# A three-part kernel on one core: queries read as whole rows of 18 tokens, keys and values in 96 partitions, weight tiles of 256 columns

## The chip, the cores and the metric

The kernel runs on one core of a Trainium2 chip. The metric is the device time of one execution in microseconds (us), and the time of a kernel is the median of its runs.

## The reference

An attention without softmax, then two feed-forward layers, over 8 batches, 8 heads, 576 tokens and 64 features (4608 tokens of 512 features). The weights are float64 in memory.

```python
kv  = einsum('bhsd,bhse->bhde', k, v)
out = einsum('bhsd,bhde->bhse', q, kv)
out = out / sqrt(mean(out * out, -1) + 1e-6) * g_norm
x   = out.transpose(0, 2, 1, 3).reshape(B * S, H * D)
h   = maximum(maximum(x @ w1, x @ w2), x @ w3)      # 512 -> 768
x   = h @ w_out                                     # 768 -> 512
g   = s * maximum(x @ w_in, 0) ** 2 + b             # 512 -> 2048
out = g @ w_out2                                    # 2048 -> 512
```

## The kernel before

**Tiling.** Tokens go in nine blocks of 512: block j below 8 holds the first N = 512 tokens of batch j, and the ninth holds the 8 x 64 tokens that are left (REM = 64 of each batch, gathered in `o_rem`). Features lie on partitions, tokens on the free axis. Heads go in four pairs p: heads p and p + 4 fill 128 partitions.

**Attention of one batch.** `load_kv` reads the first 512 tokens of k and v of a pair into 128 partitions of 4 tokens (pieces of 1 KB), `load_rem` the last 64 of all heads into `krem` and `vrem`; `kv_mm` sums k-by-v products into the PSUM tile `kvps`, 10 matmuls a pair, the last two from `krem` and `vrem`. `load_q` reads q as blocks of 32 x 32, which one DVE transpose (`q_turn`) turns into `qt`, features by tokens. Then come q times kv (`o_mm`, PSUM `ops`, `orps` for the last 64 tokens), copy and square on ACT (`o`, `sq`), the mean square (`ms_mm`), `u` on ACT and DVE (`ms_ln`, `ms_newton`), and the split of the result into a high and a low part `xh`, `xl` (`x_split`), since each product of the feed-forward layers is made of three matmuls (`mm3`).

**First layer.** 18 tiles of W1 to W3 and 6 of `w_out` are loaded as raw float64 words (`conv_load`, buffers `raw_craw` and `raw_o`) and turned into high and low parts `w_w` in three steps (`conv_unpack`, `conv_sum`, `conv_split`) on DVE, ACT and POOL. Group g (`g1_part`) multiplies a block by 128 columns of one of W1, W2, W3; three groups and a maximum make one tile of h (`g1_out`, `h_split`), and `g2_mm` multiplies h by `w_out`. The result `x1d` goes to device memory.

**Second layer.** Phase 2 runs on quarters of tokens with fewer products than a plain multiplication. `put` turns the result back into rows of tokens and stores it. For the last pair of the quarters (`qq == NQ - 1`, the tokens of `o_rem`) TensorE turns it (PSUM `turn`) and eight DMAs of 64 tokens store it, six issued by SP and two by ACT; all others go out in DMAs of 32 tokens in four parts of 128 features.

**Order.** Each step gets a position with `at(pos, step)`; a slot of the steady part is one group. SP and PE follow the positions (PE from the steady part on); the order on DVE, ACT and POOL is a scheduler's. All loads and nearly all stores are issued by SP, in order. In the start-up, the attention of batch 0, the tiles of W and the products of block 0 come together; from block 1 on the attention of the next batch runs beside the products of a block.

Of the kernel before, what the change touches and what calls it, by code (L numbers as in the profile page):

```python
# [9 lines left out]
F32 = mybir.dt.float32  # L10
# [19 lines left out]
def attention_max_ffn_relu2_ffn(ctx: ExitStack, tc, q, k, v, g_norm, w1, w2, w3, wo, wi, w2o, s, b, out):  # L30
# [21 lines left out]
    M2 = DF2 // P  # L52
    REM = S - N
    NB = B + 1
    C = N // P
    SB = S // 32
    G1 = 3 * M1
    SL = G1 + KD
    ts = nc.vector.tensor_scalar
# [5 lines left out]
    def at(pos, fn, *args):  # L65
        plan.append((pos, len(plan), fn, args))
# [15 lines left out]
    def pair(slot, nm):  # L82
        return base.tile([P, 2, N], F32R, tag=slot, name=nm)
# [52 lines left out]
    rems = {}  # L136
    for nm in "kv":
        rems[nm] = at_.tile([P, H, D], F32, name=f"{nm}rem")
        nc.gpsimd.memset(rems[nm], 0.0)
# [34 lines left out]
    def stage(raw, tr, gc):  # L174

        def parts():
            if gc == "st":
# [15 lines left out]

    def conv_split(key, slot, eng):
        f = st.pop(("f32", key))
        w = wt[key] = pair(slot, f"w_{key[0]}_{key[1]}")
        split(w[:, 0], w[:, 1], f, eng)

    def conv_store(key):
        nc.sync.dma_start(out=wd[key[1] // 4][:, key[1] % 4], in_=st.pop(("f32", key)))  # L200

    def w1_src(n):
        m, i = divmod(n, 3)
        w = (w1, w2, w3)[i][:, m * P:(m + 1) * P]
# [15 lines left out]

    def load_rem(bb):
        for nm, src in (("k", k), ("v", v)):
            nc.sync.dma_start(out=rems[nm][:REM], in_=src[bb, :, N:, :].rearrange("h r d -> r h d"))

    def load_kv(bb, p):
        for nm, src in (("k", k), ("v", v)):
            tag = (nm, 2) if bb or p < 2 else ("o", NP)
            t = st[nm, bb, p] = at_.tile([P, 2, C, D], F32, tag=tag[0], bufs=tag[1], name=f"{nm}_{bb}_{p}")  # L230
# [35 lines left out]
    def load_q(bb, p0, n):


        if p0 == 0:
            st["qraw"] = at_.tile([P, NP, SB, 32], F32, tag="qraw", name=f"qraw_{bb}")  # L270
        for j in range(P // 32):
            h = (j // 2) * NP + p0
            src = q[bb, h:h + n, :, (j % 2) * 32:(j % 2 + 1) * 32].rearrange("h (i t) f -> t (h i) f", t=32)
            nc.sync.dma_start(out=st["qraw"][j * 32:(j + 1) * 32, p0:p0 + n].rearrange("t h i f -> t (h i) f"), in_=src)

    def q_turn(bb, p):
        t = st["qt", p] = at_.tile([P, S], F32, tag="qt", bufs=2, name=f"qt_{bb}_{p}")
        nc.vector.transpose(t, st["qraw"][:, p].rearrange("p i f -> p (i f)"))
# [166 lines left out]
    for j in range(NB):  # L445
        t = SL * j
        if j + 1 < B:
            bb = j + 1
            xpb = 3 if j else 2
            if bb < 4:  # L450
                kt = us(4 + 15 * bb)
                plan_kv(bb, lambda p: kt + (2 * p - 3.9) * US, lambda p: kt + 2 * p * US)
            else:
                plan_kv(bb, lambda p: t - 4 + p - 1.9, lambda p: t - 4 + p + 0.5)
            at(max(t - 10, us(20)), load_q, bb, 0, NP)
            at(t + 0.2, kv_diag, bb)
            for p in range(NP):
                a = t + 3 * p
                at(a + 0.4, q_turn, bb, p)
                if bb:  # L460
                    at(a + 1.3, q_split, bb, p)
                at(a + 3.5, o_mm, bb, p)
                at(a + 4.3, o_out, bb, p)
                plan_norm(bb, p, a + 4.5, 0.9)
                at(t + G1 + 0.2 + 0.5 * p, x_split, bb, p, nc.gpsimd if p < xpb else nc.vector)
            at(t + 13.3, o_rems, bb)
        elif j + 1 == B:
            for p in range(NP):
                a = t + 3 * p

                def sq(p=p):
                    st["o", B, p] = o_rem[:, p, :]
                    o_sq(B, p, o_rem[:, p, :])

                at(a + 0.4, sq)
                plan_norm(B, p, a + 0.5, 0.9)
                at(t + G1 + 0.2 + 0.5 * p, x_split, B, p, nc.gpsimd if p < 3 else nc.vector)
        for g in range(G1):
            if j or g >= 4:
                at(t + g, g1_part, j, g, range(KD))  # L480
# [282 lines left out]
    def unit():  # L763
        p2["unit"] = tmp("unit")[:, :P]
        make_identity(nc, p2["unit"])

    def put(H, c, u):

        qq = H // 2
        if qq == NQ - 1:  # L770
# [18 lines left out]

# [87 lines left out]
```

## Time and profile before

| what | value |
| --- | --- |
| median of 3 runs | 1454.68 us (1452.45 to 1455.13) |
| span of the profiled execution | 1453.9 us |
| PE busy | 1396.9 us, 96% of the span |
| DVE busy | 951.2 us, 65% |
| ACT busy | 813.8 us, 56% |
| DMA, mean rate | 139 GB/s |

The profile is of one execution, and its span runs from its first to its last instruction; the run has no time of its own beside it, so the span is taken for it. It lies inside the runs, 0.8 us under the median. PE is TensorE's matmuls, DVE VectorE, ACT ScalarE, POOL GpSimd and SP the engine that issues DMAs. "DMA share" is the busy share of 16 DMA engines (packets that overlap on an engine can make it more than 1).

### The profile page before, as it was taken

How to read it: one execution, taken by the hardware profiler on the slowest of the kernel's cores; microseconds unless marked ns; L12 is line 12 of the kernel's file. 1: busy time of each engine (PE TensorE's matmuls, PEld its weight loads, DVE VectorE, ACT ScalarE, POOL GpSimd, SP SyncE). 2: the span in 40 equal slices, each digit the busy share in tenths (PEclk: the TensorE clock that was granted, in tenths of full speed). 3: DMA queues.
4: the chain of work that ended last, by engine and by line, in shares of the span. 5: the costliest groups of instructions: out<-in, count | busy, mean ns of one | idle time of the engine just before them, and what ended most of it. 6: DMA issues, size and time to landing. Idle time of an engine off the chain costs nothing. (4 is left out here: it accounts for less than half of the span.)

```text
span 1453.9 us, 19580 instructions
## 1 busy us (share of the span) xinstructions
PE 1396.9 (96%) x6860; PEld 1145.0 (79%) x6860; DVE 951.2 (65%) x1439; ACT 813.8 (56%) x1454; POOL 332.7 (23%) x238
## 2 busy tenths in 40 slices
PE   4689999999999999999999999999999999999997
PEld 2467888888878788888878778988788888888887
DVE  4899473646364636446466765756877888888785
ACT  5776454445353545443365646647676666656565
POOL 1334242324232324331100000000002414141412
PEclk9789999999999999999999999999999999999999
DMA  9986244435364742213135464453676444454541
GB/s 195 198 207 106 76 65 111 111 117 102 127 91 124 113 123 58 80 29 116 65 124 202 162 230 178 142 203 127 217 265 231 132 146 174 152 175 148 176 135 40
DMA packets 229459, 202.63 MB, mean 139 GB/s; under 512 B 126320, under 2 KB 179568, under 8 KB 227184
## 3 DMA queue, kind: packets, MB, share of 16 engines
q1 hardware_dynamic: 229200, 201.11, 48.9%
q8 instruction: 54, 0.88, 0.3%
q14 instruction: 45, 0.37, 0.1%
q10 hardware_dynamic: 160, 0.26, 0.0%
HBM read 126.88 MB, written 74.45 MB: 138 GB/s over the span
## 5 line engine op out<-in xcount | busy, mean ns | idle before, releaser
L97 PE MATMUL g<-xl,w_w 128*128 128x512 f32 x648 | 255.9, 395 | 3.8 <-POOL xl L93 3.8
L96 PE MATMUL g<-xh,w_w 128*128 128x512 f32 x648 | 257.4, 400 | 0.2 <-ACT xh L92 0.2
L98 PE MATMUL g<-xh,w_w 128*128 128x512 f32 x648 | 255.6, 395 | 0.0
L92 ACT ACTIVATE zx<-z 128x512 fp32r<-128x512 f32 (+1 forms) x280 | 161.2, 586 | 123.5 <-PE zs_a L707 35.7
L629 PE MATMUL ps_a<-x_q,w_q 128*128 128x512 f32 (+1 forms) x960 | 211.1, 371 | 2.8 <-DVE cs L537 1.7
L707 PE MATMUL zs_a<-zx,w_q 128*128 128x512 f32 (+1 forms) x960 | 203.7, 369 | 0.6 <-POOL zx L93 0.3
L93 POOL TENSOR_TENSOR zx<-z,zx 128x512 fp32r<-128x512 f32 (+1 forms) x46 | 63.3, 1376 | 593.8 <-DMA gd<-cs 381.4
L629 PEld LDWEIGHTS ps_a<-x_q,w_q 128*128 128x128 f32 x960 | 167.2, 188 | 38.0 <-DVE cs L537 3.4
L93 DVE TENSOR_TENSOR zx<-z,zx 128x512 fp32r<-128x512 f32 (+1 forms) x234 | 170.6, 746 | 34.8 <-ACT zx L92 34.3
L707 PEld LDWEIGHTS zs_a<-zx,w_q 128*128 128x128 f32 x960 | 167.8, 188 | 31.9 <-POOL zx L93 0.7
L97 PEld LDWEIGHTS g<-xl,w_w 128*128 128x128 f32 x648 | 123.3, 190 | 29.7 <-POOL xl L93 4.2
L96 PEld LDWEIGHTS g<-xh,w_w 128*128 128x128 f32 x648 | 123.2, 191 | 26.8 <-issue 1.0
L98 PEld LDWEIGHTS g<-xh,w_w 128*128 128x128 f32 x648 | 123.2, 190 | 26.3
L171 POOL TENSOR_TENSOR tr_ctr<-tr_ctr,gc_cgc 128x512 int32<-128x512 int32 x42 | 56.0, 1333 | 232.4 <-DVE gc_cgc L166 169.8
L629 PE MATMUL ps_b<-x_q,w_q 128*128 128x512 f32 (+1 forms) x480 | 107.6, 372 | 1.1 <-ACT cs L640 1.0
L707 PE MATMUL zs_b<-zx,w_q 128*128 128x512 f32 (+1 forms) x480 | 103.8, 371 | 2.2 <-DVE zx L93 2.2
L372 DVE TENSOR_TENSOR h<-g,h 128x512 f32<-128x512 f32 x108 | 73.9, 684 | 42.9 <-PE g L98 42.4
L707 PEld LDWEIGHTS zs_b<-zx,w_q 128*128 128x128 f32 x480 | 83.9, 188 | 19.1 <-DVE zx L93 3.4
L629 PEld LDWEIGHTS ps_b<-x_q,w_q 128*128 128x128 f32 x480 | 83.8, 188 | 18.9 <-ACT cs L640 1.8
L96 PE MATMUL g<-h,w_o 128*128 128x512 f32 x216 | 85.7, 397 | 0.0
L162 ACT ACTIVATE tr_ctr<-raw_craw 128x512 int32<-128x512 uint32 x42 | 28.1, 669 | 102.1 <-DMA wd<-tr_ctr 86.1
L97 PE MATMUL g<-h,w_o 128*128 128x512 f32 x216 | 84.6, 392 | 0.0
(160 smaller groups left out, 2268.3 us busy)
## 6 DMA issues: line engine op xcount, KB each, us to landing
z<-gd SPq DMA_DIRECT2D x64, 512.0 KB
gd<-cs SPq DMA_DIRECT2D x96, 256.0 KB
z<-gd SPq DMA_DIRECT2D x48, 256.0 KB
x1d<-x SPq DMA_DIRECT2D x36, 256.0 KB
k<-in_k_dram SPq DMA_DIRECT2D x32, 256.0 KB
v<-in_v_dram SPq DMA_DIRECT2D x32, 256.0 KB
raw_craw<-in_moe_w_in_dram SPq DMA_DIRECT2D x16, 512.0 KB
wd<-tr_ctr SPq DMA_DIRECT2D x32, 256.0 KB
```

The lines of the kernel that those rows point to most:

```text
L92: act(out=hi, in_=src, func=AF.Copy)
L93: eng.tensor_tensor(out=lo, in0=src, in1=hi.bitcast(F32), op=ALU.subtract)
L96: nc.tensor.matmul(ps, lhsT=w[:, 0, sl], rhs=xh, start=first, stop=False)
L97: nc.tensor.matmul(ps, lhsT=w[:, 0, sl], rhs=xl, start=False, stop=False)
L98: nc.tensor.matmul(ps, lhsT=w[:, 1, sl], rhs=xh, start=False, stop=last)
L162: act(out=r, in_=w32[:, :, 0], func=AF.Copy, scale=2.0 ** -29)
L171: nc.gpsimd.tensor_tensor(out=t, in0=t, in1=g.bitcast(I32), op=ALU.add)
L372: nc.vector.tensor_tensor(out=st["h", m], in0=ps, in1=st["h", m], op=ALU.max)
L629: nc.tensor.matmul(ps, lhsT=w[:, a, c], rhs=x[:, b_], start=new and k == 0 and e == 0, stop=k == HK - 1 and e == 2, skip_group_check=True)
L707: nc.tensor.matmul(ps, lhsT=w[:, a, c], rhs=x[:, b_, :n], start=new and k_ == 0 and e == 0, stop=k_ == 3 and e == 2, skip_group_check=True)
```

## The change

- **Queries.** One DMA for each 32 partitions reads whole rows: partition t gets tokens 18t to 18t + 17 of a head, all 64 features, 4608 bytes on end. Both halves of a head's features are needed in different partitions, so each head is read twice, the copies shifted by 32 columns, and `q_turn` picks 32 of every 64 columns. A load is now for one pair of heads, with two buffers. Tokens thereby lie in the order (c, t) with token = 18t + c, from q to the store.
- **Keys and values.** A pair's 576 tokens lie in 96 partitions of 6 tokens (pieces of 1536 bytes); `load_rem`, its buffers and the memsets on them are gone. `kv_mm` makes 12 matmuls a pair.
- **W1 to W3.** A tile holds 256 columns of half of the inputs (pieces of 2 KB), before 128 columns of all inputs (1 KB). Two groups share two tiles, the groups' order has two tiles of h side by side, and `h_split` comes for two at a time.
- **Stores.** They address memory by `tokens(bb)`, the view (c, t) of a batch: rows of neighbouring t are 18 rows (36,864 bytes) apart. The stores of 32 tokens keep their shape; those of 64 tokens become 2 x 32 rows.

```diff
 def load_kv(bb, p):
-    t = at_.tile([P, 2, C, D], F32, tag=tag[0], bufs=tag[1])
-    nc.sync.dma_start(out=t.rearrange("p h c d -> p h (c d)"),
-                      in_=src[bb, p::NP, :N, :].rearrange("h (p c) d -> p h (c d)", c=C))
+    t = pool.tile([P, 2, CK, D], F32, tag=tag, bufs=bufs)          # CK = 6, KP = 96
+    nc.sync.dma_start(out=t[:KP].rearrange("p h c d -> p h (c d)"),
+                      in_=src[bb, p::NP].rearrange("h (p c) d -> p h (c d)", c=CK))
 def load_q
-    src = q[bb, h:h + n, :, (j % 2) * 32:(j % 2 + 1) * 32].rearrange("h (i t) f -> t (h i) f", t=32)
+    nc.sync.dma_start(out=t[j * 32:(j + 1) * 32, o:o + SB * D],    # o = 32 - 32 * (j % 2)
+                      in_=q[bb, (j // 2) * NP + p].rearrange("(t c) f -> t (c f)", c=SB))
 def w1_src(n)
-    m, i = divmod(n, 3)
-    w = (w1, w2, w3)[i][:, m * P:(m + 1) * P]
+    mp, i, kh = key_of(n)
+    w = (w1, w2, w3)[i][:, 2 * mp * P:2 * (mp + 1) * P]
 def g1_part
-    mm3(..., wt["w", g], slice(kk * P, (kk + 1) * P), ...)
+    c = 2 * (kk % 2) + mm                                          # mp, i, mm = g // 6, g % 6 // 2, g % 2
+    mm3(..., wt["w", (mp, i, kk // 2)], slice(c * P, (c + 1) * P), ...)
+def tokens(bb):
+    return out[bb * S:(bb + 1) * S].rearrange("(t c) f -> c t f", c=SB)
 def put (last pair)
-    eng.dma_start(out=out[r0:r0 + REM], in_=o[e * REM:(e + 1) * REM])
+    eng.dma_start(out=tokens(4 * c + 2 * u + e)[N // 32:], in_=o[e * REM:(e + 1) * REM])
 def put (others)
-    nc.sync.dma_start(out=out[r0:r0 + 32].rearrange("r (a f) -> a r f", a=4), in_=o[:, j])
+    nc.sync.dma_start(out=tokens(2 * qq + c)[4 * u + j].rearrange("r (a f) -> a r f", a=4), in_=o[:, j])
```

On SP, the first loads of batch 0 are these, before (`k_0` and `v_0` are pair 0, `raw_craw` and `raw_o` the tiles of W; the last figures are the shape of one DMA, x4 is four DMAs):

```order
1 L231 DMA k_0_117<-in_k_dram 128x2x256
2 L231 DMA v_0_119<-in_v_dram 128x2x256
3 L225 DMA krem<-in_k_dram 64x8x64
4 L225 DMA vrem<-in_v_dram 64x8x64
5 L274 DMA qraw_123<-in_q_dram 32x18x32 x4
6 L149 DMA raw_craw<-in_moe_w_dram 64x4x128 x2
```

And these in the changed kernel:

```order
1 L228 DMA k_0_113<-in_k_dram 96x2x384
2 L228 DMA v_0_115<-in_v_dram 96x2x384
3 L268 DMA qraw_0_117<-in_q_dram 32x1152 x4
4 L145 DMA raw_craw<-in_moe_w_dram 64x2x256 x2
5 L228 DMA k_1_125<-in_k_dram 96x2x384
6 L228 DMA v_1_127<-in_v_dram 96x2x384
```

The two loads of the last 64 tokens are gone, a q load has pieces of 1152 elements where it had 18 of 32, and a tile of W has two pieces of 256 where it had four of 128.

On PE, where block 0 goes from the last group of the first layer (`g_0_17`) to the products with `w_out` (`g_0_0`, `g_0_1`), the mean square of pair 3 of batch 1 (`ms_3`) stands here before:

```order
278 L96 MATMUL g_0_17_1221<-xh_291,w_w_938 128x512
279 L328 MATMUL ms_3_1218<-sqh_3_1167,ones 128x512
280 L329 MATMUL ms_3_1218<-sql_3_1168,ones 128x512
281 L97 MATMUL g_0_17_1221<-xl_292,w_w_938 128x512
282 L98 MATMUL g_0_17_1221<-xh_291,w_w_938 128x512
283 L96 MATMUL g_0_17_1221<-xh_291,w_w_938 128x512
284 L97 MATMUL g_0_17_1221<-xl_292,w_w_938 128x512
285 L98 MATMUL g_0_17_1221<-xh_291,w_w_938 128x512
286 L96 MATMUL g_0_0_1248<-h_0_701,w_o_990 128x512
```

And here in the changed kernel:

```order
267 L99 MATMUL g_0_17_1261<-xh_296,w_w_973 128x512
268 L97 MATMUL g_0_0_1291<-h_0_782,w_o_1023 128x512
269 L98 MATMUL g_0_0_1291<-h_0_782,w_o_1023 128x512
270 L99 MATMUL g_0_0_1291<-h_0_782,w_o_1023 128x512
271 L97 MATMUL g_0_1_1295<-h_0_782,w_o_1023 128x512
272 L98 MATMUL g_0_1_1295<-h_0_782,w_o_1023 128x512
273 L324 MATMUL ms_3_1258<-sqh_3_1211,ones 128x512
274 L325 MATMUL ms_3_1258<-sql_3_1212,ones 128x512
275 L99 MATMUL g_0_1_1295<-h_0_782,w_o_1023 128x512
```

It had five matmuls of the last group behind it, and has that whole group and five matmuls with `w_out` ahead of it: ten later.

On SP, the last stores of the kernel are these, before (the stores of `o_1_3` are of 32 tokens; those of L781 are of the last pair, 64 tokens each):

```order
580 L788 DMA out_dram<-o_1_2_12113 4x32x128 x4
581 L788 DMA out_dram<-o_1_3_12139 4x32x128 x4
582 L781 DMA out_dram<-o_0_0_12545 64x512 x2
583 L781 DMA out_dram<-o_0_1_12557 64x512 x2
584 L781 DMA out_dram<-o_1_0_12622 64x512
585 L781 DMA out_dram<-o_1_1_12631 64x512
```

And these in the changed kernel:

```order
586 L786 DMA out_dram<-o_1_2_12265 4x32x128 x4
587 L786 DMA out_dram<-o_1_3_12291 4x32x128 x4
588 L780 DMA out_dram<-o_0_0_12697 2x32x512 x2
589 L780 DMA out_dram<-o_0_1_12709 2x32x512 x2
590 L780 DMA out_dram<-o_1_0_12774 2x32x512
591 L780 DMA out_dram<-o_1_1_12783 2x32x512
```

Number and place are as they were, the shape of the last six is another; the two that ACT issues change in the same way.

## Rows read from the trace of the kernel before

**Rows 1.** The page: busy time, share of the span and instructions of each engine.

```profile
PE 1396.9 (96%) x6860; PEld 1145.0 (79%) x6860; DVE 951.2 (65%) x1439; ACT 813.8 (56%) x1454; POOL 332.7 (23%) x238
```

**Rows 2.** Windows by stage: length, busy time by engine; PEclk, DMA share, GB/s.

```profile
0.00:31.30 31.30, 14.81 (x98) 8.85 (x98) 11.37 (x25) 14.24 (x28) 5.53 (x10) 1.00 0.94 189
31.30:73.30 42.00, 25.56 (x147) 16.74 (x147) 35.58 (x51) 30.69 (x53) 13.77 (x10) 0.72 1.10 204
73.30:135.90 62.60, 54.16 (x337) 42.27 (x337) 57.55 (x81) 46.40 (x83) 27.24 (x17) 0.94 0.78 169
135.90:156.60 20.70, 20.68 (x79) 16.85 (x80) 15.37 (x20) 10.00 (x17) 5.53 (x4) 0.86 0.13 34
156.60:1436.00 1279.40, 1270.54 (x6120) 1050.39 (x6120) 826.49 (x1254) 705.49 (x1260) 279.63 (x198) 1.00 0.46 137
```

**Rows 3.** Waits of PE from 145 us on: total us, times, longest.

```profile
PE zs_b L707 <- DVE zx L93: 2.2, 4, 1.4
```

**Rows 4.** Waits of DVE from 0 to 150 us, those for DMA.

```profile
DVE qt L278 <- DMA qraw<-in_q_dram: 12.9, 6, 6.6
DVE gc_o L161 <- DMA raw_o<-in_moe_w_dram: 6.4, 6, 2.4
DVE gc_cgc L161 <- DMA raw_craw<-in_moe_w_dram: 6.0, 4, 2.8
```

**Rows 5.** Timeline of PE, start-up and one batch later: start, us, instructions, idle before.

```profile
102.77 0.34 PE L243 MATMUL kvps<-vrem,krem 128*64 128x64 f32 x4 [3.17 <-DMA vrem<-in_v_dram]
...
135.92 0.79 PE L328 MATMUL ms<-sqh,ones 128*128 128x512 f32 x1 [3.39 <-DVE u L342]
...
156.64 0.39 PE L96 MATMUL g<-xh,w_w 128*128 128x512 f32 x1
156.86 0.39 PE L97 MATMUL g<-xl,w_w 128*128 128x512 f32 x1
...
285.94 0.69 PE L243 MATMUL kvps<-v,k 128*64 128x64 f32 x16
286.46 0.29 PE L243 MATMUL kvps<-vrem,krem 128*64 128x64 f32 x4
```

**Rows 6.** Timeline of DVE: last q_turn of batch 0, last split of block 1's input.

```profile
26.51 0.78 DVE L278 STREAM_TRANSPOSE qt<-qraw 128x576 f32<-128x576 f32 x1 [1.17 <-DMA qraw<-in_q_dram]
...
151.55 0.69 DVE L93 TENSOR_TENSOR xl<-o,xh 128x512 fp32r<-128x512 f32 x1
```

**Rows 7.** Windows of one kind of transfer each; columns as in rows 2.

```profile
103.00:105.00 2.00, 2.00 (x11) 1.60 (x8) 2.00 (x5) 0.59 (x2) 0.00 (x0) 0.77 1.03 378
94.00:96.00 2.00, 2.00 (x11) 1.65 (x10) 1.90 (x4) 1.37 (x4) 0.00 (x0) 1.00 1.07 225
131.00:133.00 2.00, 1.53 (x7) 0.94 (x5) 2.00 (x2) 1.55 (x3) 1.13 (x1) 1.00 1.61 132
156.30:158.30 2.00, 2.00 (x11) 1.65 (x10) 0.00 (x0) 0.36 (x1) 0.00 (x0) 1.00 0.70 255
1199.00:1200.00 1.00, 1.00 (x6) 0.82 (x5) 0.00 (x0) 0.46 (x1) 0.47 (x1) 1.00 1.07 436
1402.00:1406.00 4.00, 4.00 (x36) 4.00 (x35) 2.79 (x9) 2.18 (x6) 0.99 (x1) 1.00 0.28 83
1441.30:1444.00 2.70, 2.45 (x18) 2.15 (x18) 1.43 (x4) 1.82 (x4) 0.00 (x0) 1.00 0.82 191
1450.10:1452.60 2.50, 0.00 (x0) 0.00 (x0) 0.00 (x0) 0.20 (x1) 0.00 (x0) 0.95 0.78 209
```

**Rows 8.** Timeline of the tail: the last stores and the last copy.

```profile
1440.10 10.69 SPq L781 DMA_DIRECT2D out_dram<-o  x6
...
1449.71 0.60 ACT L776 ACTIVATE o<-turn 128x512 f32<-128x512 f32 x1 [0.77 <-PE turn L773]
1450.34 0.50 ACTq L781 DMA_DIRECT2D out_dram<-o  x1
```

More of the change, by code (lines that the diff above doesn't have):

```diff
@@ L54, in attention_max_ffn_relu2_ffn @@
     NB = B + 1
-    C = N // P
     SB = S // 32
+    CK = 6
+    KP = S // CK
     G1 = 3 * M1
@@ L135, in attention_max_ffn_relu2_ffn @@
     o_rem = at_.tile([P, NP, N], F32, name="o_rem")
[L136 to L139, printed above, removed]
     st = {}
@@ L186, in stage, with key_of @@
                 parts)
+    def key_of(n):
+        return ((0, 0, 0), (0, 1, 0), (0, 0, 1), (0, 1, 1))[n] if n < 4 else (n // 6, n % 6 // 2, n % 2)
     W1S = [f"w{n}" for n in range(G1)]
@@ L195, in conv_split @@
         f = st.pop(("f32", key))
-        w = wt[key] = pair(slot, f"w_{key[0]}_{key[1]}")
+        w = wt[key] = pair(slot, f"w_{slot}")
         split(w[:, 0], w[:, 1], f, eng)
@@ L202, in w1_src @@
     def w1_src(n):
-        m, i = divmod(n, 3)
-        w = (w1, w2, w3)[i][:, m * P:(m + 1) * P]
-        return [(h * D, D, w[h * NP * D:(h + 1) * NP * D, :].rearrange("(k d) c -> d k c", d=D)) for h in range(2)]
+        mp, i, kh = key_of(n)
+        w = (w1, w2, w3)[i][:, 2 * mp * P:2 * (mp + 1) * P]
+        return [(h * D, D, w[(h * NP + 2 * kh) * D:(h * NP + 2 * kh + 2) * D, :].rearrange("(k d) c -> d k c", d=D))
+                for h in range(2)]
     def p2_src(n):
@@ L219, in p2_src @@
                 for kk in range(2) for b in range(2)]
-    def load_rem(bb):
-        for nm, src in (("k", k), ("v", v)):
-            nc.sync.dma_start(out=rems[nm][:REM], in_=src[bb, :, N:, :].rearrange("h r d -> r h d"))
     def load_kv(bb, p):
-        for nm, src in (("k", k), ("v", v)):
-            tag = (nm, 2) if bb or p < 2 else ("o", NP)
-            t = st[nm, bb, p] = at_.tile([P, 2, C, D], F32, tag=tag[0], bufs=tag[1], name=f"{nm}_{bb}_{p}")
-            nc.sync.dma_start(out=t.rearrange("p h c d -> p h (c d)"),
-                              in_=src[bb, p::NP, :N, :].rearrange("h (p c) d -> p h (c d)", c=C))
+        for e, (nm, src) in enumerate((("k", k), ("v", v))):
+            pool, tag, bufs = (at_, nm, 2) if bb or p < 2 else (base, HS[2 * (p - 2) + e], 1)
+            t = st[nm, bb, p] = pool.tile([P, 2, CK, D], F32, tag=tag, bufs=bufs, name=f"{nm}_{bb}_{p}")
+            nc.sync.dma_start(out=t[:KP].rearrange("p h c d -> p h (c d)"),
+                              in_=src[bb, p::NP].rearrange("h (p c) d -> p h (c d)", c=CK))
     def kv_mm(bb, p):
@@ L238, in kv_mm @@
         k_, v_ = st.pop(("k", bb, p)), st.pop(("v", bb, p))
-        for c in range(C + 1):
+        for c in range(CK):
             for h in range(2):
-                kc, vc = ((k_[:, h, c, :], v_[:, h, c, :]) if c < C else
-                          (rems["k"][:, p + h * NP, :], rems["v"][:, p + h * NP, :]))
-                nc.tensor.matmul(ps[h * D:(h + 1) * D, p, :], lhsT=kc, rhs=vc, start=(c == 0), stop=(c == C))
+                nc.tensor.matmul(ps[h * D:(h + 1) * D, p, :], lhsT=k_[:KP, h, c, :], rhs=v_[:KP, h, c, :],
+                                 start=(c == 0), stop=(c == CK - 1))
     def kv_out(bb):
@@ L264, in kv_diag, with load_q @@
         st["kvhl"] = (kvh, kvl)
[L266 to L270 removed]
+    def load_q(bb, p):
+        t = st["qraw", p] = at_.tile([P, SB * D + 32], F32, tag="qraw", bufs=2, name=f"qraw_{bb}_{p}")
         for j in range(P // 32):
[L272 to L274 removed]
+            o = 32 - 32 * (j % 2)
+            nc.sync.dma_start(out=t[j * 32:(j + 1) * 32, o:o + SB * D],
+                              in_=q[bb, (j // 2) * NP + p].rearrange("(t c) f -> t (c f)", c=SB))
     def q_turn(bb, p):
         t = st["qt", p] = at_.tile([P, S], F32, tag="qt", bufs=2, name=f"qt_{bb}_{p}")
[L278 removed]
+        raw = st.pop(("qraw", p))[:, 32:].rearrange("p (c x) -> p c x", x=D)
+        nc.vector.transpose(t.rearrange("p (c t) -> p c t", t=32), raw[:, :, :32])
     def q_split(bb, p):
@@ L392, in plan_kv @@
     def plan_kv(bb, load, mm):
-        at(mm(0) - 2.9 * US, load_rem, bb)
         for p in range(NP):
@@ L412, in plan_conv @@
         a, pr, gc = stages[n % 3] if n < G1 else stages_o[n % 2 if n < G1 + 5 else 0]
-        key = ("w", n) if n < G1 else ("o", n - G1)
+        key = ("w", key_of(n)) if n < G1 else ("o", n - G1)
         src = w1_src(n) if n < G1 else [(0, P, wo[(n - G1) * P:(n - G1 + 1) * P, :])]
@@ L418, in plan_conv @@
         at(pos + 2 * d, conv_split, key, W1S[n] if n < G1 else WOS[n - G1], nc.vector)
-    first = {nm: us(0.01 * n) for n, nm in enumerate("kv0 rem q0 w0 kv1 q1 w1 kv2 q2 w2 kv3 q3 s".split())}
+    first = {nm: us(0.01 * n) for n, nm in enumerate("kv0 q0 w0 kv1 q1 w1 kv2 q2 w2 kv3 q3 s".split())}
     for p in range(NP):
@@ L424, in attention_max_ffn_relu2_ffn @@
         at(us(4.6 + 2 * p), kv_diag_pair, p)
-        at(first[f"q{p}"], load_q, 0, p, 1)
-    at(first["rem"], load_rem, 0)
+        at(first[f"q{p}"], load_q, 0, p)
     at(first["s"], load_scalars)
@@ L454, in attention_max_ffn_relu2_ffn @@
                 plan_kv(bb, lambda p: t - 4 + p - 1.9, lambda p: t - 4 + p + 0.5)
-            at(max(t - 10, us(20)), load_q, bb, 0, NP)
             at(t + 0.2, kv_diag, bb)
@@ L458, in attention_max_ffn_relu2_ffn @@
                 a = t + 3 * p
+                at(max(t - 10 if p < 2 else a - 5.4, us(20)), load_q, bb, p)
                 at(a + 0.4, q_turn, bb, p)
@@ L481, in attention_max_ffn_relu2_ffn @@
             at(t + max(g, j == 0 and 3 or 0) + 1.01, g1_out, j, g)
-            if g % 3 == 2:
-                at(t + max(g, j == 0 and 3 or 0) + 1.25, h_split, j, g // 3)
+            if g % 6 > 3:
+                at(t + max(g, j == 0 and 3 or 0) + 1.25, h_split, j, 2 * (g // 6) + g % 2)
         for n in range(KD):
```

8 lines of the change are left out of this document (4 added, 4 removed).

## The prediction

> **What bounds the kernel now.** I read the page first: PE is busy for 1396.9 of 1453.9 us [rows 1]. The windows by stage say where the other 57 us lie [rows 2]. From 156.6 to 1436 PE stands idle for 1279.40 − 1270.54 = 8.9 us, and its waits there are crumbs, the largest group 2.2 us in four times [rows 3]. Whatever the change does to transfers in that long stretch is covered by matmuls; there only matmuls that come or go count. The idle time is ahead of it, 16.5 us before 31.3, 16.4 us to 73.3 and 8.4 us to 135.9, and in the tail. So the change is priced in three places: start-up, matmuls of the dense part, tail.
>
> The three pieces of the start-up have different limits. Up to 31.3 us the DMA engines are 0.94 busy and move 189 GB/s, while DVE works 11.4 of 31.3 us: transfers set the pace. From 31.3 to 73.3 both are full (DMA 1.10, DVE 35.6 of 42.0). From 73.3 to 135.9 DVE is busy 57.6 of 62.6 us and sets it [rows 2]. Of DVE's waits 12.9 + 6.4 + 6.0 = 25.3 us are for q and tiles of W [rows 4].
>
> **Tail.** The last eight stores are of 64 tokens x 2 KB = 131 KB each, 1.05 MB in all. Before, four go at 191 GB/s from 1441.3 to 1444 (191 x 2.7 = 0.52 MB, all four), and the last four at 209 GB/s from 1450.1 to 1452.6, with the engines 0.82 and 0.78 busy: about 13 of 16 [rows 7]. The span ends 1453.9 − 1452.6 = 1.3 us later. Now their outer dimension is 2. What a small outer dimension does, the kernel shows in its other stores, 4 x 32 x 128: in a stretch with little else the share is 0.28, that is 4.5 of 16 engines, at 83 GB/s, 18.5 GB/s for each busy one [rows 7]. By this pattern 2 x 32 x 512 goes on two engines. An engine with 2-KB pieces moves 255/(0.70 x 16) = 22.8 GB/s (the load at 156.3), with mixed larger ones 436/(1.07 x 16) = 25.5 [rows 7]. I take 22.8, since the pieces are the same: two engines move 45.5 GB/s, and 1.05 MB takes 23.0 us. The first stores are issued at 1440.10 as before and their data start at 1441.3; the second half is ready at 1449.71 + 0.60 = 1450.3 at the latest [rows 8], when the first half (11.5 us, to 1452.8) still fills both engines, so nothing runs dry. End: 1441.3 + 23.0 + 1.3 = 1465.6, **+11.7 us**. With 25.5 GB/s an engine it is +9.3, with 18.5 (28.3 us) +17.0, with the 14.6 that each engine does in the last stores now (191/(0.82 x 16)) 35.9 us and +24.6; with all engines still in use it is 0. Nothing hides it: no engine has work behind it.
>
> The Trainium skill says the same as a rule ("DMA: Bandwidth & Descriptors", on why a DMA increments its semaphore by 16): a DMA is spread over the largest number of engines up to 16 that divides the outermost dimensions of both its sides, 16 for 64 rows and 2 for 2 x 32. By that rule the tail is the sum above; the share of 0.28 at an outer 4 agrees, and no run here shows an outer 2 yet.
>
> The other stores keep 4 parts and only get a pitch of 36,864 bytes. Should that make each piece half as fast, they end later, but the last of them is issued some 20 us ahead of the tail under matmuls: nothing.
>
> **Matmuls of the dense part.** `kv_mm` goes from 20 to 24 records a pair (each product shows as two). Sixteen start at 285.94, the next at 286.46: 0.52/16 = 32.5 ns each [rows 5], so 4 more are 0.13 us. Four batches, 16 pairs, lie after 156.6: 16 x 0.13 = **+2.1 us**, 0 if fewer partitions make them shorter, 4.2 at double. The groups of W multiply the same shapes as before, only at other columns: nothing.
>
> **Start-up.** Per pair of batch 0, three transfers before the next q_turn:
> - q moved 295 KB in 128-byte pieces; such a load runs at 132 GB/s [rows 7], 2.2 us. Now it reads 590 KB. With long pieces at the best rate, 436, it is 1.35 us; at the 225 GB/s of the W loads, whose two DMAs also write only 64 partitions each, 2.6 us [rows 7]. −0.9 to +0.4. I take the slow end, for 32 partitions are nearer to 64 than to 128, and the W load has 8 times longer pieces than q and still not the rate of k and v.
> - k and v moved 524 KB at 378 GB/s, 1.4 us; now 590 KB, 1.6 us at that rate, 2.1 us at three quarters of it (96 of 128 partitions). +0.2 to +0.7; I take +0.4.
> - W moves 524 KB either way. At 225 GB/s it is 2.3 us; if the 1-KB pieces were the limit and 2 KB ran at 436, 1.2 us. −1.1 to 0; I take 0, since k and v have 1-KB pieces too and run at 378, so that pieces of that length aren't what holds W [rows 7].
> - The two loads of the last tokens (262 KB once, 256-byte pieces) go: between 132 and 378 GB/s 2.0 to 0.7 us, −1.3.
>
> A rule of the Trainium skill stands against the hope in the long pieces ("SBUF — State Buffer", Door 1, the DMA port swizzle): 32 or 64 partitions reach half of the 16 ports, some 218 GB/s, whatever the pieces. The row of W at 225 agrees. By the rule q takes 2.7 us a pair, by the row 2.6.
>
> Four pairs: 4 x (0.4 + 0.4) − 1.3 = +1.9 us, so the last q_turn, at 26.51 before [rows 6], comes near 28.4. Bounds: 4 x (−0.9 + 0.2 − 1.1) − 2.0 = −9.2 and 4 x (0.4 + 0.7) − 0.7 = +3.7.
>
> What comes of that at 156.64, where block 1 begins? PE's two waits on the way are 3.17 us for `vrem` at 102.77, which is gone, and 3.39 us for DVE's `u` at 135.92 [rows 5]. The first gain only makes PE earlier at the second wait, as DVE sets that. But `ms_3`, which waits there, now stands ten matmuls later, and these fill 10 x 0.22 = 2.2 us of it (156.86 − 156.64 [rows 5]). DVE itself is late by the +1.9 of above, less what its idle time takes: 6.4 us between 31.3 and 73.3, 5.0 us to 135.9 [rows 2], partly the `vrem` wait passed on. I let it keep 0.3 of the 1.9. So block 1 begins 2.2 − 0.3, about **2 us earlier**. DVE's last split for block 1 ends at 152.24 [rows 6], 4.4 us before 156.64, and isn't late. Bounds: −9.2 − 2.2 = −11.4 with all transfers at the fast end, and +3.7 + 2.2 = +6 if `ms_3` waits as long as before at its new place.
>
> **Sum.** 1453.9 + 11.7 + 2.1 − 2 = 1465.7 against the profiled execution; the median lies 0.8 us above its span, so 1466 us, +0.8%. A difference under 0.2% (2.9 us) is no change to the measurement.
>
> **Rivals.**
> - *The last stores still use all engines* (an outer 2 is folded with the 32 inside). The share of 0.28 at an outer 4 speaks against it, though there the part of 128 features lies inside and can't be folded. Then −2 + 2.1: 1454.8, no change; with the fast start-up up to 9 us faster.
> - *Faster: the start-up hangs on transfers and long pieces free it.* DVE waits 25.3 us for q and W [rows 4]; if that is DVE's pace to 156.64 and q and W arrive in time, all of it goes, and the sum is 13.8 − 25.3: 1443. It decides from 16.7 us of gain in the start-up (13.8 + 2.9). Against it: the W row at 225 GB/s, the doubled bytes of q, and DVE's own work of 57.6 in 62.6 us, which no transfer shortens. In between (about −14) it cancels the tail.
> - *Two slow engines:* 14.6 GB/s each, 1453.9 + 24.6 + 0.1 + 0.8: 1479.
> - *A new wait in the dense part:* tiles of h now end two at a time. If PE waits in each of 9 blocks for a second split, by the 0.69 of a split on DVE [rows 6] or double that, 6 to 12 us come on top: up to 1478. Against it: the products with `w_out` begin with the first tile, and at three matmuls of 0.22 us for each of two outputs per tile the sixth is due 5 x 6 x 0.22 = 6.6 us after the first.
>
> **How the numbers follow.** Two engines with a small start-up effect 0.68 (1459 to 1473 by the bounds of rate and start-up that I hold likely); two slow engines 0.07; new waits 0.05; these three are slower, 0.80. All engines 0.12: 0.08 no change, 0.04 faster. Freed start-up 0.08: 0.06 faster, 0.02 no change. Faster 0.10, no change 0.10, slower 0.80. The range 1451 to 1476 takes in the case of all engines and the tail at 17 us, and leaves out the freed start-up and the slowest cases.
>
> **What would show it.** In the tail: a DMA share near 0.12 and some 45 GB/s from 1441 on, and the end 21 to 24 us after the first store's data; a share near 0.8 refutes it. In the start-up: no wait for `vrem`, the first q_turn earlier than now for lack of the 262 KB, the last one near 28 us, W and q loads near 220 GB/s; rates near 400 would show the piece length to be the limit and bring the second rival. At block 1: its first matmul near 154.6. In the dense part: 128 more records of `kvps`, PE busy +4 us in all, and idle time after 156 still below 10 us. The forecast is wrong by most if the tail takes all engines.

## The result, and the profile after

The changed kernel takes 1468.76 us (median of 4 runs, 1467.79 to 1469.34), the kernel before 1454.91 us in the runs beside it: ratio 1.0095, 95% interval 1.0081 to 1.0110, slower by some 13.8 us. The forecast was 1466 us. The profiled execution has a span of 1466.7 us, 12.8 more than before; as a run it took 1469.34 us, 2.6 more than its span, and the other three runs took 1.8 to 2.5 us more than theirs.

The windows of the changed kernel, with the columns of [rows 2]: the first 31.3 us, the dense part, the last stores, and three kinds of transfer of the start-up (k and v at 10, q at 12, W at 15).

```profile
0.00:31.30 31.30, 16.16 (x114) 9.31 (x115) 12.40 (x27) 16.43 (x32) 4.52 (x8) 0.89 0.95 216
...
156.60:1436.00 1279.40, 1271.49 (x6174) 1052.60 (x6173) 819.38 (x1253) 701.56 (x1257) 274.95 (x197) 1.00 0.45 143
...
1442.00:1444.00 2.00, 1.75 (x15) 1.57 (x13) 0.68 (x3) 0.81 (x3) 0.00 (x0) 1.00 0.09 15
...
1442.00:1452.00 10.00, 7.29 (x54) 6.41 (x52) 2.21 (x6) 4.00 (x9) 0.00 (x0) 1.00 0.12 39
...
1454.00:1464.00 10.00, 0.00 (x0) 0.00 (x0) 0.00 (x0) 0.00 (x0) 0.00 (x0) 0.54 0.13 51
...
10.00:11.00 1.00, 1.00 (x2) 0.34 (x1) 0.43 (x1) 0.69 (x2) 0.00 (x0) 1.00 1.10 263
...
12.00:14.00 2.00, 1.06 (x20) 1.09 (x22) 0.44 (x1) 1.55 (x4) 1.26 (x1) 1.00 0.98 215
...
15.00:16.00 1.00, 1.00 (x2) 0.00 (x0) 0.57 (x1) 0.00 (x0) 0.00 (x0) 1.00 1.04 230
```

In the tail 0.12 to 0.13 of 16 engines are busy, that is two, where 0.82 and 0.78 were [rows 7]. The timeline of the changed kernel has the same steps as [rows 8], with one new wait: ACT waits 1.55 us for an earlier store out of `o` before it makes the last copy:

```profile
1441.26 11.51 SPq L780 DMA_DIRECT2D out_dram<-o  x6
...
1451.64 0.60 ACT L776 ACTIVATE o<-turn 128x512 f32<-128x512 f32 x1 [1.55 <-DMA out_dram<-o]
1452.26 0.53 ACTq L780 DMA_DIRECT2D out_dram<-o  x1
```

From the first of the last stores to the end it takes 1466.7 − 1441.26 = 25.4 us, before 1453.9 − 1440.10 = 13.8: 11.6 us of the 12.8 lie here. The rest lies between block 1's first matmul, which comes when it came before (156.61; 156.64 in [rows 5]), and that first store: 1284.6 us, before 1283.5. The pair of `kvps` that [rows 5] show at 285.94 takes 0.84 us to the next matmul; before, 20 records at the pace of [rows 5] (0.52 us for 16) take 0.65, and the next matmul comes after 0.73, at 286.67.

The timeline of PE in the changed kernel, with two new waits of the start-up, block 1's first matmul and that pair:

```profile
108.78 0.92 PE L238 MATMUL kvps<-v,k 96*64 96x64 f32 x24 [2.88 <-DMA v<-in_v_dram]
...
112.48 1.55 PE L238 MATMUL kvps<-v,k 96*64 96x64 f32 x24 [2.78 <-DMA v<-in_v_dram]
...
156.61 0.39 PE L97 MATMUL g<-xh,w_w 128*128 128x512 f32 x1
...
286.30 0.92 PE L238 MATMUL kvps<-v,k 96*64 96x64 f32 x24
287.14 0.50 PE L97 MATMUL g<-h,w_o 128*128 128x512 f32 x1
```

PE's waits for keys and values in the start-up, in all, times and the longest; first before the change, then after:

```profile
PE kvps L243 <- DMA v<-in_v_dram: 12.3, 8, 4.5
PE kvps L243 <- DMA vrem<-in_v_dram: 4.8, 3, 3.2
```

```profile
PE kvps L238 <- DMA v<-in_v_dram: 26.1, 8, 5.7
```

And DVE's timeline in the changed kernel, the q turns of pairs 0 and 3 of batch 0:

```profile
8.25 0.78 DVE L274 STREAM_TRANSPOSE qt<-qraw 128x576 f32<-128x576 f32 x1 [6.49 <-DMA qraw<-in_q_dram]
...
29.62 0.78 DVE L274 STREAM_TRANSPOSE qt<-qraw 128x576 f32<-128x576 f32 x1 [1.90 <-DMA qraw<-in_q_dram]
```

The wait for `vrem` and that for `u` at `ms_3` are gone, but new ones for v stand in the same stretch. All of PE's waits together, to 160 us, fell from 41.4 to 38.7 us in these two traces, so the waits for v took the place of others. The last q turn comes 3.1 us later than in [rows 6].

### The profile page after: what moved, and what is told of

Its sections match the earlier page's. It is cut to its first block, busy times and chain, and to the rows that moved or that the text cites. A ratio compares the mean times of both kernels' runs of the same rounds, so it can differ in the third digit from the quotient of the medians.

```text
span 1466.7 us, 19910 instructions
## 1 busy us (share of the span) xinstructions
PE 1401.6 (96%) x6988; PEld 1151.0 (78%) x6988; DVE 945.3 (64%) x1439; ACT 811.6 (55%) x1454; POOL 326.7 (22%) x236
## 5 line engine op out<-in xcount | busy, mean ns | idle before, releaser
L98 PEld LDWEIGHTS g<-xl,w_w 128*128 128x128 f32 x648 | 123.9, 191 | 26.1 <-POOL xl L94 0.6
L157 DVE TENSOR_SCALAR gc_cgc<-raw_craw 128x512 uint16<-128x512 uint16 x42 | 22.4, 534 | 120.1 <-DMA raw_craw<-in_moe_w_out_dram 57.2
L97 PE MATMUL g<-h,w_o 128*128 128x512 f32 x216 | 85.3, 396 | 1.5 <-DVE h L371 1.5
```

The source lines that it names most:

```text
L97: nc.tensor.matmul(ps, lhsT=w[:, 0, sl], rhs=xh, start=first, stop=False)
L98: nc.tensor.matmul(ps, lhsT=w[:, 0, sl], rhs=xl, start=False, stop=False)
L157: ts(out=c, in0=w16[:, :, 3], scalar1=0x7FFF, scalar2=None, op0=ALU.bitwise_and)
```

## The experiments

The start-up is not the same in each execution. In the kernel `before_tail2` below, whose start-up is the kernel before's line by line, block 1 begins at 153.47, against 156.64 in [rows 5]. The start-up of the changed kernel, which `after_tail32` and `q_two` below share, began block 1 at 156.61, 154.97 and 153.85. So a single profile tells nothing of effects on block 1's begin under some 3 us; they are read from the ratios.

**The stores alone, first way.** In the changed kernel each of the last eight stores is cut in two of 32 rows, at the same pitch:

```diff
-eng.dma_start(out=tokens(4 * c + 2 * u + e)[N // 32:], in_=o[e * REM:(e + 1) * REM])
+for i in range(2):
+    eng.dma_start(out=tokens(4 * c + 2 * u + e)[N // 32 + i],
+                  in_=o[e * REM + 32 * i:e * REM + 32 * (i + 1)])
```

> The changed kernel with each of its last eight stores cut in two DMAs of 32 rows, so that the outermost dimension is 32 and not 2; the pitch of 36,864 bytes stays. Theory 1 (the number of engines of a store makes the tail): the DMA share of the tail goes from 0.12 to 0.7 or more, the end comes some 14 to 15 us after the first of the last stores is issued (25.4 in the changed kernel, 13.8 before), the span 1455 to 1456.5 and the ratio to the kernel before 1.000 to 1.002. Rival (the pitch of 36,864 bytes makes the stores slow): the tail stays over 20 us and the time near 1468.

Ratio to the kernel before 1.0022 (1.0013 to 1.0032). Two windows on these stores in its trace; the span is 1452.9:

```profile
1440.00:1443.00 3.00, 2.75 (x22) 2.45 (x21) 1.43 (x4) 1.82 (x4) 0.00 (x0) 1.00 0.56 143
1448.00:1451.00 3.00, 0.00 (x0) 0.00 (x0) 0.00 (x0) 0.60 (x1) 0.00 (x0) 1.00 0.63 174
```

The timeline has their issue by SP:

```profile
1438.59 11.33 SPq L781 DMA_DIRECT2D out_dram<-o  x12
```

The share is 0.56 to 0.63, somewhat under the 0.7 expected, and the tail takes 1452.9 − 1438.59 = 14.3 us. The pitch stays and the tail is within 0.5 us of the 13.8 before, so the pitch is no obstacle worth more than that. Between the two ratios lie 0.73%, or 10.6 us.

**The stores alone, second way.** In the kernel before, two stores are joined into one whose outermost dimension is 2, with rows on end in memory:

```diff
-for e in range(2):
-    eng = nc.scalar if c and e else nc.sync
-    r0 = (4 * c + 2 * u + e) * S + N
-    eng.dma_start(out=out[r0:r0 + REM], in_=o[e * REM:(e + 1) * REM])
+eng = nc.scalar if c and u else nc.sync
+b0 = 4 * c + 2 * u
+eng.dma_start(out=out.rearrange("(b s) f -> b s f", s=S)[b0:b0 + 2, N:], in_=o)
```

> The kernel before with its last eight stores joined in pairs: four DMAs of 2 batches x 64 rows, the same bytes to the same places, rows on end in memory, but an outermost dimension of 2. Theory 1: two engines at some 45 GB/s, share 0.12, about 23 us for the stores, so 1453.9 + 11.6 = 1465 to 1467, ratio 1.007 to 1.009. Rival (pitch): rows are on end, so no change, 1454 to 1456.

Ratio 1.0056 (1.0037 to 1.0075), less than expected. Two windows in its tail, its begin and what follows, show the two engines; the span is 1459.4:

```profile
1436.00:1438.00 2.00, 1.75 (x14) 1.49 (x13) 0.95 (x3) 0.95 (x3) 0.00 (x0) 1.00 0.12 25
...
1440.00:1450.00 10.00, 3.29 (x25) 2.71 (x23) 0.78 (x2) 2.29 (x4) 0.00 (x0) 0.89 0.13 51
```

And the issue of the stores in its timeline:

```profile
1434.99 9.38 SPq L780 DMA_DIRECT2D out_dram<-o  x3
```

From the first issue to the end it is 1459.4 − 1434.99 = 24.4 us, 10.6 more than before; the ratio by itself is 8.2 us, with 5.4 to 10.9 in its interval, which holds the 10.6. The bytes have the places they had, so the outermost dimension alone makes this tail.

**The three parts alone.** Each is the kernel before with some of the change's own lines, which the diff ahead of the prediction shows: `q_only` with those of `load_q`, `q_turn`, `tokens` and `put` (last stores in 32 rows, as above); `w_only` with those of `key_of`, `w1_src`, `g1_part`, `g1_out` and `h_split`; `kv_only` with those of `load_kv` and `kv_mm`, and without `load_rem`; `kv_w` with the W part and the part of keys and values together. Of W, for instance:

```diff
-w = (w1, w2, w3)[i][:, m * P:(m + 1) * P]
+w = (w1, w2, w3)[i][:, 2 * mp * P:2 * (mp + 1) * P]
```

> The kernel before with the queries' part alone (whole rows of 18 tokens, read twice), the last stores in DMAs of 32 rows so that the tail is not in it; keys, values and W as before. Theory 1 (32 or 64 partitions at about 215 GB/s bound the load, the doubled bytes eat the gain of the long pieces): the q turns of batch 0 come 1 to 3 us later than before at the last, block 1 begins within 2 us of 156.6, time 1454 to 1457. Rival (the long pieces free the DMA engines for the rest): block 1 begins 3 us or more earlier, time under 1452.

> The kernel before with the tiles of W alone changed (256 columns by half of the inputs, groups in the new order). Theory 1 (64 partitions bound the load of a tile, not the 1-KB pieces): windows on W loads still show 208 to 235 GB/s, block 1 begins within 1.5 us of 156.6, the new 1.5 us wait for the maximum at the first product with w_out is there, time 1453 to 1457. Rival (2-KB pieces are faster): W at 300 GB/s or more, the start-up 3 us or more shorter, time under 1452.

> The kernel before with the keys and values alone changed (96 partitions of 6 tokens, no loads of the last 64 tokens). If the three parts add up, it is what is left of +0.22% after +0.43% for q and -0.25% for W: +0.04%, that is ratio 0.999 to 1.002. Theory: the dense part is 1.2 to 2 us longer for 128 more records of kvps, and the start-up gives about as much back. Rival (96 partitions are slow to load and k and v hold PE): ratio over 1.003, with waits for v longer than before.

> Keys, values and W changed, the queries, the order of the tokens and all stores as before. If the parts add up: -0.25% + 0.04%, ratio 0.996 to 0.999, faster than both kernels. Rival (the gain of W needs the old order of k and v, or the parts meet in the same wait): 1.000 or more.

| kernel | ratio to before | 95% interval | change in us, of 1452 |
| --- | --- | --- | --- |
| q_only | 1.0043 | 1.0028 to 1.0057 | +6.2 |
| w_only | 0.9975 | 0.9963 to 0.9987 | −3.6 |
| kv_only | 1.0020 | 1.0009 to 1.0031 | +2.9 |
| kv_w | 1.0002 | 0.9992 to 1.0013 | +0.3 |
| all three, stores of 32 rows | 1.0022 | 1.0013 to 1.0032 | +3.2 |

The parts add up within their intervals (6.2 − 3.6 + 2.9 = 5.5 against 3.2; 2.9 − 3.6 = −0.7 against 0.3). The queries cost more than the 0 to 3 us expected; some 0.5 us of it is the tail of stores of 32 rows, by that of `after_tail32`. W gains where nothing was expected, although its rate hardly moves, as expected (a window of `w_only` on W has 227 GB/s). Keys and values cost more than the +0.04% that was left for them, at the upper end of the range expected.

**The bytes of q.** `q_half` is `q_only` with half of each row, so that a pair is 295 KB as before the change, in pieces of 2304 bytes (half of the tokens are used twice, the others are left out):

```diff
-nc.sync.dma_start(out=t[j * 32:(j + 1) * 32, o:o + SB * D],
-                  in_=q[bb, (j // 2) * NP + p].rearrange("(t c) f -> t (c f)", c=SB))
+nc.sync.dma_start(out=t[j * 32:(j + 1) * 32, o:o + SB // 2 * D],
+                  in_=q[bb, (j // 2) * NP + p].rearrange("(t c) f -> t (c f)", c=SB)[:, :SB // 2 * D])
```

> The queries' part alone as in q_only, but each row is read and turned only in its first 9 tokens, used twice (so the output is wrong): 288 KB a pair, what the kernel before reads, in pieces of 2304 bytes, with the same DMAs, buffers and order; one more DVE instruction a pair. Theory 1 (the doubled bytes at some 215 GB/s cost the +0.43%): ratio 0.996 to 1.000, last q turn of batch 0 at 23 to 26 us. Rival (the order of the loads, one pair at a time with two buffers, costs it): ratio still over 1.003.

Ratio 0.9934 (0.9922 to 0.9946): 1.09% or 16 us under q_only, more than any theory had said. The last q turn of batch 0 is at 23.85, 5.4 us earlier than q_only's 29.27. Block 1's first matmul, `q_only` first and then `q_half`, comes 16.0 us earlier, so the gain lies in the start-up:

```profile
160.09 0.39 PE L96 MATMUL g<-xh,w_w 128*128 128x512 f32 x1
```

```profile
144.11 0.39 PE L96 MATMUL g<-xh,w_w 128*128 128x512 f32 x1
```

Per pair 295 KB less at 215 GB/s are 1.4 us, and ten pairs (batches 0 and 1, half of 2) are loaded ahead of block 1: 14 us, an estimate. So here a microsecond of q's transfers saved in the start-up gives about one of time.

`q_half` is also 0.66%, 9.6 us, faster than the kernel before, with the same bytes of q and, for batch 0, the same four DMAs of 32 partitions a pair. Batch 0's last q turn is at 23.85 where it was at 26.51. For q, then, long pieces do pay as long as nothing is read twice. Windows that hold q and little else, before (128-byte pieces), and in `q_half` (2304 bytes):

```profile
11.40:13.10 1.70, 0.70 (x10) 0.54 (x11) 1.38 (x2) 1.32 (x2) 0.11 (x1) 1.00 1.36 169
```

```profile
10.90:11.50 0.60, 0.52 (x3) 0.33 (x1) 0.59 (x1) 0.58 (x1) 0.00 (x0) 1.00 1.07 262
```

In `q_half` the later batches' loads also go pair by pair; what that part gives was not tried alone.

**Two queues.** Here the upper 64 partitions are loaded by a DMA that ACT issues: q of batches 5 to 7 in `q_two` (on the changed kernel with stores of 32 rows, one execution), and W from the fourth tile on in `w_act` (on `w_only`). The edit of `q_two`:

```diff
-nc.sync.dma_start(out=t[j * 32:(j + 1) * 32, o:o + SB * D],
+eng = nc.scalar if j >= 2 and bb >= 5 else nc.sync
+eng.dma_start(out=t[j * 32:(j + 1) * 32, o:o + SB * D],
```

> The changed kernel with stores of 32 rows; the q loads of the upper 64 partitions of batches 5 to 7 (in the dense part, where nothing waits for them) are issued by ACT, those of the lower 64 by SP, so that both halves are written at once. Theory 1 (which partitions a transfer writes bounds it at some 215 GB/s): a window on such a load shows well over 250 GB/s, up to 400, with the packets shorter. Rival (the source rows or the engines bound it): it stays at 200 to 230 GB/s. The time stays within 0.3% of the kernel with stores of 32 rows.

> The W part alone, with the upper 64 partitions of each tile of W from the fourth one on loaded by a DMA that ACT issues, so that both halves of the partitions can be written at once and SP issues 15 DMAs fewer. Theory (the partitions written bound such a load): where both queues load W together the rate goes over 260 GB/s (230 with SP alone), ratio 0.994 to 0.997. Rival (the rows of the source or the engines bound it, and ACT's queue is only held up): the rate stays at 230, ratio 0.998 to 1.003.

Windows of `q_two`, one with both halves of a pair, one with one half (and other loads):

```profile
529.60:532.00 2.40, 2.40 (x12) 1.97 (x12) 0.69 (x1) 1.19 (x2) 0.00 (x0) 1.00 0.99 260
535.00:536.50 1.50, 1.50 (x9) 1.23 (x8) 0.43 (x1) 0.00 (x0) 0.00 (x0) 1.00 1.01 292
```

And a window of `w_act` in its W loads:

```profile
30.00:34.00 4.00, 2.39 (x4) 1.17 (x4) 1.03 (x3) 2.12 (x6) 0.00 (x0) 1.00 1.00 221
```

`q_two` took 1453.88 us. Its 260 with both halves is not above the 292 beside it, and the window of W stays at 221. `w_act` is slower, 1.0024 (1.0012 to 1.0036) against the 0.9975 of `w_only`. ACT issues at moments of its own, and in the trace of `w_act` the halves go mostly one after the other, so neither tells whether two halves at once would be faster.

**One DMA over 128 partitions.** Whether the partitions or the source bound a load of W is told apart by pairing heads 2p and 2p + 1 in place of p and p + 4. The rows of W of a pair then lie on end, and a tile of the same shape and pieces goes in one DMA. The places of k, v and q in memory change with it, and q of later batches is loaded pair by pair (lines not shown):

```diff
-return [(h * D, D, w[h * NP * D:(h + 1) * NP * D, :].rearrange("(k d) c -> d k c", d=D)) for h in range(2)]
+return [(0, P, w.rearrange("(k d) c -> d k c", d=P))]
-in_=src[bb, p::NP, :N, :]
+in_=src[bb, 2 * p:2 * p + 2, :N, :]
-h = (j // 2) * NP + p0
+h = 2 * p0 + j // 2
```

> The kernel before with the heads paired as 2p and 2p + 1 in place of p and p + 4. The rows of W that belong to a pair then lie on end, and a tile of W (still 128 columns, 1-KB pieces, the same bytes) is loaded by one DMA into 128 partitions in place of two into 64 each; q of batches 1 to 7 goes in 16 DMAs of one pair instead of 4. Theory (how many partitions one DMA writes sets its rate): windows on W loads show 300 to 378 GB/s in place of 208 to 225, a tile takes 1.5 us and not 2.4, block 1 begins 4 us or more earlier, ratio 0.993 to 0.997. Rival (the float64 rows with a pitch of 6 KB are slow at the source): W stays under 240 GB/s, ratio 0.998 to 1.002.

> As pairs, with the W part of the change on top: tiles of 256 columns by half of the inputs (2-KB pieces), one DMA of 128 partitions a tile. Theory: a rate of 350 GB/s or more on W, the gains of pairs and of w_only (0.25%) add up: ratio 0.990 to 0.995, faster than both kernels. Rival (source): 230 to 260 GB/s as in w_only, ratio 0.996 to 0.999; if DVE, not the transfers, holds the start-up once W comes faster, about the ratio of pairs.

`pairs` takes 1444.38 us, ratio 0.9954 (0.9941 to 0.9966): faster than both kernels. `pairs_w` takes 1445.98 us, 0.9962 (0.9948 to 0.9975), no better. Windows of `pairs`, on W loads and on the third stage of [rows 2]:

```profile
26.00:30.00 4.00, 2.48 (x5) 0.88 (x4) 2.77 (x6) 2.75 (x5) 0.00 (x0) 1.00 1.08 363
...
73.30:135.90 62.60, 57.75 (x319) 45.94 (x319) 62.14 (x86) 45.07 (x82) 24.76 (x16) 0.95 0.53 137
```

Block 1's first matmul in its timeline:

```profile
146.61 0.39 PE L96 MATMUL g<-xh,w_w 128*128 128x512 f32 x1
```

The same 1-KB pieces of the same matrix go at 363 GB/s where the row of [rows 7] had 225: what held W is that one DMA writes only 64 partitions, not the source and not the pieces; nor is it the size of a DMA, for k and v, 262 KB each over 128 partitions, go at 350 GB/s in `pairs` (13.95 to 15.40 us). This is shown for the rate; the 0.46% of time belong to the whole edit. From 73.3 on DVE is now busy 62.14 of 62.60 us and the DMA engines 0.53, so DVE has next to nothing left to give there. The same two windows of `pairs_w`:

```profile
26.00:30.00 4.00, 1.56 (x4) 0.59 (x4) 2.58 (x6) 2.56 (x5) 0.00 (x0) 1.00 1.05 395
...
73.30:135.90 62.60, 56.03 (x316) 44.41 (x317) 59.29 (x82) 45.48 (x82) 25.23 (x18) 0.97 0.55 133
```

W comes faster still and the time stays. That fits the last case of its expectation, DVE as the bound, but no run here made DVE's work less, so it is not shown.

**q of batch 0 once.** `w_q0` is `w_only` with each head of batch 0 read once into 32 partitions, and four DVE instructions of 32 partitions a pair in place of one (the stores of batch 0 follow the order of its tokens):

```diff
+for i in range(2):
+    lo = 64 * i + 32 * (p % 2)
+    raw = r[lo:lo + 32].rearrange("p (c x) -> p c x", x=D)
+    for x in range(2):
+        to = 64 * i + 32 * x
+        nc.vector.transpose(t[to:to + 32].rearrange("p (c t) -> p c t", t=32), raw[:, :, 32 * x:32 * x + 32])
```

> The W part alone, and of the queries' part only this: batch 0's q is read in whole rows of 18 tokens, but each head once (two DMAs of 32 partitions a pair, 295 KB), and four DVE instructions of 32 partitions move the halves to their partitions in place of one of 128. Batches 1 to 7 as before. Theory (transfers set the first 31 us, and q_half showed that the same bytes in long pieces are cheaper): q takes about 1.4 us a pair where it took 2.2, the last q turn comes 2 to 3 us earlier than in w_only (26.04), and the ratio is 0.994 to 0.997, under w_only's 0.9975. Rival (the three more DVE instructions a pair, about 2.1 us on the way from q to its matmul, eat it): 0.997 or more.

Ratio 1.0026 (1.0013 to 1.0039), so the rival holds, and by more than it said. Each small instruction takes as long as the large one (3.12 us for four), as its timeline of DVE shows:

```profile
25.98 0.43 DVE L161 TENSOR_SCALAR gc_cgc<-raw_craw 128x512 uint16<-128x512 uint16 x1 [1.63 <-DMA raw_craw<-in_moe_w_dram]
26.44 3.12 DVE L298 STREAM_TRANSPOSE qt<-qraw 32x576 f32<-32x576 f32 x4
```

A window in its start-up, and one of `w_only` just behind its loads of q:

```profile
21.00:24.00 3.00, 3.00 (x24) 1.23 (x22) 3.00 (x5) 2.33 (x4) 1.32 (x1) 1.00 0.65 138
```

```profile
24.00:27.00 3.00, 2.21 (x24) 1.78 (x23) 1.47 (x3) 3.00 (x6) 1.27 (x1) 1.00 0.42 33
```

The last q turn is not earlier (26.44 against 26.04), though it did not wait for q: on DVE it stands behind a tile of W (25.98), which waited 1.63 us for its load, and DVE is full in the window at 21. The fall of the DMA engines to 0.65 in that window need not be DVE's doing, for `w_only` has the like at 24 with DVE half idle. What makes up the 0.5% against `w_only` was not tried apart.

## Why the prediction was right, and where not

**Tail.** Forecast +11.7 us, in the trace +11.6, by the ratio to `after_tail32` +10.6. The cause is the one named, two engines, by a DMA whose outermost dimension is 2; both experiments show it, each with the other suspect, the pitch, held fixed. The rate was taken as 22.8 GB/s an engine. It is 25.5 (51 for two) from 1454 on, which was given as the upper case, and 39 for both over the first ten us, so that the two errors about cancel: the size of the tail came out this close by luck. Both kernels begin slowly, with 15 GB/s in the first 2 us of data here and 25 in `before_tail2`; that one is at 51 four us after its begin, the changed kernel only after some ten, and why is open. The Trainium skill's rule on the number of engines ("DMA: Bandwidth & Descriptors", on why a DMA increments its semaphore by 16) agrees: a share of 0.13, that is 2.1 of 16 engines, at an outermost 2.

**Dense part.** Forecast +2.1. The record pair measured 0.84 − 0.73 = 0.11 us, x 16 pairs = 1.8. From block 1 to the first last store it is 1.2 us longer in the two profiles; the same stretch takes 1434.99 − 153.47 = 1281.5 in `before_tail2`, 2 us less than before with the same code, so the sum can't be told closer. No stretch of PE filled with new waits: PE stands idle for 1279.40 − 1271.49 = 7.9 us from 156.6 to 1436, before 8.9, so the rival that h tiles two at a time stall each block did not come.

**Start-up.** Forecast −2, and here a step failed. What remains of the change with stores of 32 rows is +3.2 us (1.9 to 4.6 by the interval); less 1.8 for the dense part and 0.5 for the tail that is left, the start-up is some 0.9 us longer (−0.4 to +2.3), where 2 us shorter was forecast. The steps:
- q and k, v: from one q turn to the next it takes (29.62 − 8.25)/3 = 7.1 us, before (26.51 − 8.38)/3 = 6.0. That is +1.1 and not +0.8, and the last q turn came at 29.62, forecast 28.4. Two rows were not what the sum took them for. The row at 103 that stood for k and v (378 GB/s) is a mixture: 122 of its 401 packets, two thirds of the bytes, are 4-KB pieces of another load (`in_moe_w_out_dram`). In the start-up k and v went at 281 GB/s before and at 255 after, 1.9 and 2.3 us, so the +0.4 is right with both its ends too low. And q did not take 2.2 us before: at the 169 GB/s shown above it is 1.7, and 2.6 after at 227, +0.9 where +0.4 stood.
- W: taken at 0, it measured −3.6 us on its own. The rate hardly moves (230 against 225), and which of its parts gains, pieces, order of the groups or sharing of tiles, was not tried apart.
- "I let it keep 0.3 of the 1.9" is the step that failed. DVE's idle time was thought to swallow late transfers. `q_half` shows q's transfers going into the time nearly one for one, and in the changed kernel PE's waits for v, k's partner, grew from 12.3 + 4.8 (v and `vrem`) to 26.1 us. The sum also counts the four pairs of batch 0 alone, where ten pairs of q come ahead of block 1: the other six stand in no term. How much of each pair comes through was not measured pair by pair; ten times +0.9 are 9 us, and `q_only` cost 6.2, of which W's 3.6 give a part back.
- `vrem` and `ms_3`: both waits went as said. Waits of 2.88 and 2.78 us for v at 108.78 and 112.48 took their place.

The packets of the row at 103, a window on k and v before, and two after, k and v first, then q:

```profile
DMA packets 401, 0.76 MB, mean 378 GB/s; under 512 B 28, under 2 KB 279, under 8 KB 401
```

```profile
9.50:11.30 1.80, 1.80 (x4) 0.77 (x4) 0.43 (x1) 0.59 (x2) 0.00 (x0) 1.00 1.07 281
```

```profile
16.10:18.30 2.20, 2.20 (x5) 1.03 (x4) 1.20 (x4) 0.79 (x2) 0.00 (x0) 1.00 1.10 255
...
18.40:20.90 2.50, 0.75 (x24) 0.78 (x24) 1.20 (x2) 2.48 (x5) 0.71 (x1) 1.00 1.05 227
```

**Sum.** Of the 2.8 us between 1466 and the median of 1468.76, 1.0 lies in the span (1465.7 forecast, 1466.7) and most of the rest in the last step: the median was put 0.8 us above the span, and here it lies 2.1 above it.

That long pieces would free the start-up, the rival on the faster side, was rightly held unlikely for this change, but its mechanism was close to the truth: the start-up does hang on transfers, and `q_half` gained 9.6 us on the kernel before with long pieces of q. For W the piece is not what makes a load fast (225 GB/s at 1 KB, 227 at 2 KB), but the partitions that one DMA writes. The prediction took that from a likeness between rows; `pairs` shows it. The port rule of the Trainium skill ("SBUF — State Buffer", Door 1) has 32 and 64 partitions reach half of the ports, at about 218 GB/s, and 128 all of them. The changed kernel's windows on q and W, 215 and 230 GB/s, are close to that figure, and the 363 of `pairs` at 128 partitions agrees with more ports; the 262 of `q_half`, whose DMAs write 32 partitions each, lies above the figure.

## What to carry to other kernels

Look at the outermost dimension of every store, above all of the last ones: a layout that looks harmless can put a megabyte on two engines, and at the end nothing hides it; cut by its inner dimension, the same store cost one more issue and 0.5 us of the tail here. For loads on the critical path with pieces of 1 KB, spread one DMA over all 128 partitions before lengthening its pieces; pieces of 128 bytes are worth lengthening, but not at the price of reading the bytes twice. Before a row stands for a kind of transfer, look at the sizes of its packets. And before a stretch with idle time on an engine is taken to swallow a delay, ask whether that idle time is itself the wait for what is late.

## What the runs showed of the hardware beyond expectation

- A DVE transpose of 32 partitions x 576 took as long as one of 128 x 576 (3.12 us for four, 0.78 each).
- Loads of 96 partitions in pieces of 1.5 KB ran at 255 to 263 GB/s, a load of 128 partitions in pieces of 1 KB at 363.
- The same start-up code, in two executions, began block 1 at 153.47 and 156.64 us.
